# One product of seven by a second level of Strassen's scheme in the gate and up stage of a gated MLP

## The chip, the cores and the metric

The kernel runs on one core of a Trainium2 chip. A core has five engines that run side by side, each through its own instructions in order: TensorE (PE in the profile; matmuls, and weight loads that overlap them), VectorE (DVE), ScalarE (ACT), GpSimd (POOL) and SyncE (SP, which issues transfers here). They wait for one another by semaphores. The metric is the device time of one run, in microseconds (us), lower is better.

## The reference

Two layers on x of 2048 rows and 1024 columns: a local attention, then a gated MLP. Only the second matters here (F = 3584):

```python
def _B_ref(x, w_gate, w_up, w_down):
    g = jnp.einsum("bsd,df->bsf", x, w_gate)
    u = jnp.einsum("bsd,df->bsf", x, w_up)
    h = g * u
    return jnp.einsum("bsf,fd->bsd", h, w_down)
...
h = x + _A_ref(_layernorm(x, axis=-1), A_wqkv, A_wo)
h2 = h + _B_ref(_layernorm(h, axis=-1), B_w_gate, B_w_up, B_w_down)
```

## The kernel before

The rows are cut into 4 chunks of 512 (TC). For chunks 0 and 1, gate and up are plain products. Chunks 2 and 3 are taken together, in 14 blocks (NP) of 256 columns of gate and of up each. In a block, for gate (i = 0) and for up (i = 1), the product of a 256 x 1024 piece of weights with the 1024 x 1024 activations of the two chunks is done by Strassen's scheme in Winograd's form: both are seen as 2 x 2 cells, and seven products of cells take the place of eight. A cell of weights is 128 x 512, a cell of activations 512 x 512, so that one such product is 4 matmuls of 128 x 128 weights with 512 columns, summed in one PSUM bank. Gate and up together are 14 products, or 56 matmuls, a block.

The sums of weight cells are made a block ahead. VectorE scales and converts the raw weights to f16 (`wt`), and GpSimd makes four sums for gate and four for up from them (`sw`). For the first block VectorE makes the sums. The sums of activation cells (t1 to t4) are made once. Names in the profile carry the tile and the block: `px`, `py`, `pz`, `pv` are PSUM banks of the products, `p` is p5, `hq...` and `up` are the results for gate and up, `ws` is `wt`, `prodx` holds t1 to t4.

```python
    def weight_sums(n, eng=nc.gpsimd):
        raw = pair["w", n]
        wt = wpool.tile([128, KO, 2, 256], F16, tag="w", name=f"ws_{n}")
        if n == 0:
            nc.scalar.activation(wt[:], raw[:], ACTF.Copy, scale=scale_gu.s)
        else:
            nc.vector.tensor_scalar(wt[:], raw[:], scale_gu.s, None, ALU.mult)
        sw = wpool.tile([128, 2, 4, 4, 128], F16, tag="w", name=f"sw_{n}")
        for i in ((slice(0, 2),) if eng is nc.vector else (slice(0, 1), slice(1, 2))):
            a11, a21, a12, a22 = (wt[:, k:k + 4, i, c:c + 128].rearrange("p k i c -> p i k c")
                                  for k in (0, 4) for c in (0, 128))
            eng.tensor_tensor(sw[:, i, 0], a21, a22, ALU.add)
            eng.tensor_tensor(sw[:, i, 1], sw[:, i, 0], a11, ALU.subtract)
            eng.tensor_tensor(sw[:, i, 2], a11, a21, ALU.subtract)
            eng.tensor_tensor(sw[:, i, 3], a12, sw[:, i, 1], ALU.subtract)
        pair["a", n], pair["s", n] = wt, sw
        state["live"] += 1

    def activation_sums(l2, l3, room):
        b11, b12, b21, b22 = l2[:, 0:4, :], l3[:, 0:4, :], l2[:, 4:8, :], l3[:, 4:8, :]

        t1, t2, t3, t4 = (room[:, bass.ts(i, 4), :].bitcast(F16) for i in range(4))
        nc.vector.tensor_tensor(t1, b12, b11, ALU.subtract)
        nc.vector.tensor_tensor(t2, b22, t1, ALU.subtract)
        nc.vector.tensor_tensor(t3, b22, b12, ALU.subtract)
        nc.vector.tensor_tensor(t4, b21, t2, ALU.subtract)
        pair["b"] = (b11, b21, t1, t2, t3, t4, b22)

    def product(ps, lhs, rhs, fresh):
        for ko in range(4):
            nc.tensor.matmul(ps[:], lhsT=lhs[:, ko, :], rhs=rhs[:, ko, :], start=(fresh and ko == 0),
                             stop=(ko == 3), skip_group_check=not fresh)

    def pair_block(n, hts, sums=()):
        b11, b21, t1, t2, t3, t4, b22 = pair["b"]
        wt, sw, inv = pair["a", n], pair["s", n], scale_gu.inv
        gu = range(2)
        out = [hts, [t1k.tile([128, TC], BF, tag="t1k", name=f"up{n}_{k}")[:] for k in range(4)]]

        def bank(k, i):
            return psum.tile([128, TC], F32, tag="mm", name=f"p{k}{n}_{i}")

        xb, yb, zb, vb, p5 = [[None] * 2 for _ in range(5)]
        for i in gu:
            xb[i] = bank("x", i)
            product(xb[i], wt[:, 0:4, i, 0:128], b11, True)
            yb[i] = bank("y", i)
            nc.scalar.copy(yb[i][:], xb[i][:])
        for i in gu:
            vb[i] = bank("v", i)
            product(vb[i], sw[:, i, 0], t1, True)
            p5[i] = att.tile([128, TC], F32, tag=("lg", "t3")[i], name=f"p5{n}_{i}")
            nc.scalar.activation(p5[i][:], vb[i][:], ACTF.Copy, scale=inv)
            product(yb[i], sw[:, i, 1], t2, False)
            zb[i] = bank("z", i)
            nc.scalar.copy(zb[i][:], yb[i][:])
        for i in gu:
            product(zb[i], sw[:, i, 2], t3, False)
            nc.vector.scalar_tensor_tensor(out[i][3], zb[i][:], inv, p5[i][:], ALU.mult, ALU.add)
            product(xb[i], wt[:, 4:8, i, 0:128], b21, False)
            nc.scalar.activation(out[i][0], xb[i][:], ACTF.Copy, scale=inv)
            for k in sums[2 * i:2 * i + 2]:
                k()
        for i in gu:
            product(zb[i], wt[:, 4:8, i, 128:256], t4, False)
            nc.scalar.activation(out[i][2], zb[i][:], ACTF.Copy, scale=inv)
            product(yb[i], sw[:, i, 3], b22, False)
            nc.vector.scalar_tensor_tensor(out[i][1], yb[i][:], inv, p5[i][:], ALU.mult, ALU.add)
        for k in (3, 0, 2, 1):
            nc.vector.tensor_tensor(out[0][k], out[0][k], out[1][k], ALU.mult)
        state["live"] -= 2
```

The scheme runs on three partial results that are passed on: x, then y (a copy of x plus the t2 product), then z (a copy of that y plus the t3 product). The product `v` (`sw[:, i, 0]` with t1) goes into SBUF as p5 and is added when a result that needs it leaves PSUM. The loop around it:

```python
    for n in range(NP):
        if n + 1 < NP:
            weight_sums(n + 1)
            if n + 2 < NP:
                load_pair(n + 2)
            else:
                names = ("b11a", "b12a", "b21a", "b21b", "b12b")
                ws = {k: home(wpool, "w", "dn_" + k, BF) for k in names}
                down["b11"] = [ws["b11a"], home(att, "oD", "dn_b11b", BF)]
                down["b12"] = [ws["b12a"], ws["b12b"]]
                down["b21"] = [ws["b21a"], ws["b21b"]]
                load_down(down["b11"], 0, 0)
                load_down(down["b12"], 0, 1)
        else:
            load_down(down["b21"], 1, 0)
        sums = [] if n == 0 else [
            (lambda n=n, k=k: abs_sum_h(n - 1, k, h23[4 * (n - 1) + k])) for k in range(4)]
        pair_block(n, h23[4 * n:4 * n + 4], sums)
        if n == NP - 2:
            conv_down(down["b11"])
```

A buffer pool hands a place out again when the last reader of it is done. An engine that needs a place waits for that reader.

Of the kernel before, what the change touches and what calls it, by code (L numbers as in the profile page):

```python
# [9 lines left out]
F32 = mybir.dt.float32  # L10
I32 = mybir.dt.int32
F16 = mybir.dt.float16
ALU = mybir.AluOpType
ACTF = mybir.ActivationFunctionType
# [11 lines left out]
TC = 512  # L26
NCH = S // TC
SUB = TC // 4
KO = D // 128
NF = F // 128  # L30
NP = NF // 2
# [47 lines left out]
def kernel(  # L79
# [11 lines left out]
    nc = tc.nc  # L91
    x = A_x.flatten_outer_dims()
# [12 lines left out]
    att = ctx.enter_context(tc.tile_pool(name="att", bufs=1))  # L105
# [687 lines left out]
    pair = {}  # L793
# [8 lines left out]
# [5 lines that stand above are left out]
        else:  # L807
            nc.vector.tensor_scalar(wt[:], raw[:], scale_gu.s, None, ALU.mult)
        sw = wpool.tile([128, 2, 4, 4, 128], F16, tag="w", name=f"sw_{n}")
        for i in ((slice(0, 2),) if eng is nc.vector else (slice(0, 1), slice(1, 2))):  # L810
            a11, a21, a12, a22 = (wt[:, k:k + 4, i, c:c + 128].rearrange("p k i c -> p i k c")
                                  for k in (0, 4) for c in (0, 128))
            eng.tensor_tensor(sw[:, i, 0], a21, a22, ALU.add)  # L813
            eng.tensor_tensor(sw[:, i, 1], sw[:, i, 0], a11, ALU.subtract)  # L814
            eng.tensor_tensor(sw[:, i, 2], a11, a21, ALU.subtract)  # L815
            eng.tensor_tensor(sw[:, i, 3], a12, sw[:, i, 1], ALU.subtract)  # L816
        pair["a", n], pair["s", n] = wt, sw
        state["live"] += 1

# [10 lines left out]
    def product(ps, lhs, rhs, fresh):  # L830
        for ko in range(4):
            nc.tensor.matmul(ps[:], lhsT=lhs[:, ko, :], rhs=rhs[:, ko, :], start=(fresh and ko == 0),  # L832
                             stop=(ko == 3), skip_group_check=not fresh)

    def pair_block(n, hts, sums=()):
        b11, b21, t1, t2, t3, t4, b22 = pair["b"]
        wt, sw, inv = pair["a", n], pair["s", n], scale_gu.inv
# [4 lines that stand above are left out]
            return psum.tile([128, TC], F32, tag="mm", name=f"p{k}{n}_{i}")  # L842

        xb, yb, zb, vb, p5 = [[None] * 2 for _ in range(5)]
        for i in gu:
            xb[i] = bank("x", i)
            product(xb[i], wt[:, 0:4, i, 0:128], b11, True)
            yb[i] = bank("y", i)
            nc.scalar.copy(yb[i][:], xb[i][:])  # L849
        for i in gu:  # L850
            vb[i] = bank("v", i)
            product(vb[i], sw[:, i, 0], t1, True)
            p5[i] = att.tile([128, TC], F32, tag=("lg", "t3")[i], name=f"p5{n}_{i}")
            nc.scalar.activation(p5[i][:], vb[i][:], ACTF.Copy, scale=inv)
            product(yb[i], sw[:, i, 1], t2, False)
            zb[i] = bank("z", i)
            nc.scalar.copy(zb[i][:], yb[i][:])
        for i in gu:
            product(zb[i], sw[:, i, 2], t3, False)
            nc.vector.scalar_tensor_tensor(out[i][3], zb[i][:], inv, p5[i][:], ALU.mult, ALU.add)  # L860
            product(xb[i], wt[:, 4:8, i, 0:128], b21, False)
            nc.scalar.activation(out[i][0], xb[i][:], ACTF.Copy, scale=inv)
            for k in sums[2 * i:2 * i + 2]:
                k()
        for i in gu:
            product(zb[i], wt[:, 4:8, i, 128:256], t4, False)
            nc.scalar.activation(out[i][2], zb[i][:], ACTF.Copy, scale=inv)
            product(yb[i], sw[:, i, 3], b22, False)
            nc.vector.scalar_tensor_tensor(out[i][1], yb[i][:], inv, p5[i][:], ALU.mult, ALU.add)
        for k in (3, 0, 2, 1):  # L870
            nc.vector.tensor_tensor(out[0][k], out[0][k], out[1][k], ALU.mult)
        state["live"] -= 2
# [239 lines left out]
    b11, b21 = ([wts["dn", n, a] for a in range(2)] for n in ("11", "21"))  # L1112

    def halves(parts, name):
        return [pool.tile([128, KO, TC], BF, tag=tag, name=f"{name}{i}") for i, (pool, tag) in enumerate(parts)]

    b12 = halves(((att, "qD"), (att, "kD")), "b12")
    a21 = halves(((lnTp, "lnT"), (lnTp, "lnT")), "a21")
    a22 = halves(((lnTp, "lnT"), (wpool, "w")), "a22")
# [121 lines left out]
    b22 = halves(((lnTp, "lnT"), (wpool, "w")), "b22")  # L1241
# [15 lines left out]
    t2 = halves(((wpool, "w"), (wpool, "w")), "t2_")  # L1257
# [5 lines left out]
    for q in range(4):  # L1263
        ev = psum.tile([128, TC], F32, tag="mm", name=f"ev{q}")
        dprod(ev, q, FS1, fcells(b11), True)
        p = lnp.tile([128, TC], F32, tag="ln", name=f"ep5_{q}")
# [7 lines left out]
    room = wpool.tile([128, 4, TC], F32, tag="w", name="hsr0")  # L1274
# [4 lines left out]
    b21 = halves(((lnTp, "lnT"), (lnTp, "lnT")), "b21r")  # L1279
# [10 lines left out]
    a22 = halves(((att, "vD"), (att, "oD")), "a22r")  # L1290
# [42 lines left out]
    t4 = t2  # L1333
# [11 lines left out]
    retire(2)  # L1345
    load_pair(1)
    weight_sums(0, nc.vector)
    for q in range(4):
        dprod(zs[q], q, F22, fcells(t4), False)
# [20 lines left out]
# [20 lines that stand above are left out]
# [16 lines left out]
    for q in range(4):  # L1406
        dprod(ps_x[q], q, HA["11"], fcells(down["b11"]), True)
        if q == 1:
            scale_h.total(ps_y[3])
            inv = const.tile([128, 1], F32, name="inv_hd")  # L1410
            nc.vector.tensor_tensor(inv[:], scale_h.inv, scale_d.inv, ALU.mult)
            inv = inv[:]
# [26 lines left out]
    p5 = []  # L1439
    for q in range(4):  # L1440
        dprod(ps_x[q], q, S1, fcells(t1h), True)
        p = lnp.tile([128, TC], F32, tag="ln", name=f"dp5_{q}")
# [60 lines left out]
```

## Time and profile before

| | us |
|---|---|
| median of 3 runs | 766.32 |
| lowest and highest | 766.16, 766.51 |
| span of the profiled run | 764.4 |
| PE busy | 756.2 |
| VectorE busy | 627.9 |
| ScalarE busy | 531.5 |
| GpSimd busy | 144.9 |

How to read the views that follow. A line of groups or of the timeline has the engine, the line of the kernel (L), the operation, what it writes and reads (`out<-in`), partitions x elements and type. In the timeline the first two numbers are the start and the length in us, neighbours of one kind are merged (x4), and square brackets tell how long the engine had been idle before, and who ended that. A row of windows gives the busy time of each engine in a stretch. The matmuls of a stream overlap: one with 512 columns is recorded with 379 ns, and the next starts 215.8 ns after it. So it is the spacing of the starts, not the recorded length, that says what a matmul costs.

The stage that is changed begins at 506.6 us (first `px`) and its last product is issued by 675.9 us, where the first `dx` product of the down stage starts.

### The profile page before, as it was taken

To read this page: it belongs to the slowest core of one execution; us is meant where nothing else is said; L and a number is where in the kernel's file an instruction comes from. 1 tells how busy PE (TensorE), PEld (TensorE's weight loads), DVE (VectorE), ACT (ScalarE), POOL (GpSimd) and SP (SyncE) were. 2 spreads that over 40 slices of the span, in tenths; PEclk is the share of its full clock that TensorE was granted. 3 is DMA by queue.
4 is the path that set the end of the run, shared out by engine and by line. 5 is a ranking of instruction groups with operands and counts; after the bars stand their busy time and mean duration, and the time that the engine had idled before them with its cause. 6 is when DMAs were issued, how large, how long until landed. Compare 5 with 4: busy or idle time off the path is not lost.

```text
span 764.4 us, 10272 instructions
## 1 busy us (share of the span) xinstructions
PE 756.2 (99%) x3576; PEld 348.0 (46%) x3632; DVE 627.9 (82%) x758; ACT 531.5 (70%) x1010; POOL 144.9 (19%) x155
## 2 busy tenths in 40 slices
PE   8999999999999999999999999999999999999998
PEld 6444444444444444444444444444444444444444
DVE  6879999999999999999999999976554453578862
ACT  4756864556799598997798984846767677788230
POOL 0010000200002000010000001018778778600000
PEclk9999999999999999999999999999999999999999
DMA  8999695967998959879768528684242332830001
GB/s 272 255 237 263 183 287 131 301 191 172 343 345 283 302 178 294 271 245 336 245 214 275 174 95 280 150 206 128 57 110 62 105 94 72 275 112 27 1 28 55
DMA packets 194099, 146.29 MB, mean 191 GB/s; under 512 B 83968, under 2 KB 184192, under 8 KB 192000
## 3 DMA queue, kind: packets, MB, share of 16 engines
q1 hardware_dynamic: 184640, 117.99, 54.6%
q0 software_dynamic: 3728, 22.02, 8.4%
q10 hardware_dynamic: 5680, 5.64, 2.3%
q8 instruction: 28, 0.46, 0.2%
q14 instruction: 23, 0.19, 0.1%
HBM read 111.02 MB, written 27.26 MB: 181 GB/s over the span
## 4 chain that ended last, share of the span: by engine, by line
PE 86%; DVE 8%; ACT 2%; DMA 1%; issue 1%; ACTq 0%; DVEq 0%; SPq 0%
PE ps L474 17%; PE dx L1093 6%; PE pz L832 6%; PE pwu L474 6%; PE py L832 6%; PE px L832 6%; PE pwg L474 6%; PE wo L1147 4%; PE pv L832 3%; PE ey L1093 3%; PE ez L1093 3%; PE ex L1093 3%; PE dy L1093 3%; PE pu L474 2%; PE pg L474 2%; DVE prod L531 2%
## 5 line engine op out<-in xcount | busy, mean ns | idle before, releaser
L474 PE MATMUL ps<-lnT,w_qkv 128*128 128x512 bf16 x595 | 131.1, 379 | 0.7
L474 PEld LDWEIGHTS <-w_qkv 128*128 128x128 bf16 (+1 forms) x608 | 59.3, 98 | 71.5
L531 DVE TENSOR_TENSOR prod<-qD,kD 128x4096 bf16<-128x4096 bf16 (+1 forms) x34 | 72.3, 2160 | 4.0 <-DMA kD<-kd 4.0
L579 DVE TENSOR_TENSOR pv<-vD,at 128x4096 bf16<-128x4096 bf16 x32 | 72.4, 2286 | 0.3
L832 PEld LDWEIGHTS <-sw 128*128 128x128 f16 x448 | 43.8, 98 | 53.0 <-issue 0.2
L474 PEld LDWEIGHTS <-w_wg 128*128 128x128 bf16 x448 | 43.8, 98 | 52.9
L474 PEld LDWEIGHTS <-w_wu 128*128 128x128 bf16 x448 | 43.7, 98 | 52.9
L388 ACT CAST sg<-ps 128x512 bf16<-128x512 f32 x72 | 41.6, 584 | 30.7 <-PE ps L474 26.1
L832 PE MATMUL px<-lnT,ws 128*128 128x512 bf16 x212 | 53.1, 379 | 0.6
L474 PE MATMUL pg<-lnT,w_wg 128*128 128x512 bf16 x219 | 52.7, 379 | 0.3
L474 PE MATMUL pwu<-lnT,w_wu 128*128 128x512 bf16 x220 | 52.6, 379 | 0.3
L474 PE MATMUL pu<-lnT,w_wu 128*128 128x512 bf16 x220 | 52.6, 379 | 0.2
L474 PE MATMUL pwg<-lnT,w_wg 128*128 128x512 bf16 x219 | 52.3, 379 | 0.2
L832 PEld LDWEIGHTS <-ws 128*128 128x128 f16 x336 | 32.8, 98 | 39.7
L592 POOL DMA_DIRECT2D od<-oD x4 | 2.2, 542 | 249.4 <-DVE oD L590 249.4
L813 POOL TENSOR_TENSOR sw<-ws 128x512 f16<-128x512 f16 x26 | 30.0, 1153 | 78.4 <-PE pz L832 47.2
L1093 PEld LDWEIGHTS <-gs 128*128 128x128 f16 (+1 forms) x280 | 27.3, 98 | 33.2 <-DVE gs L1261 0.5
L533 DVE TENSOR_TENSOR prod<-prod 128x4096 bf16<-128x4096 bf16 x16 | 36.6, 2288 | 0.3
L849 ACT COPY py<-px 128x512 f32<-128x512 f32 x28 | 16.0, 570 | 24.2 <-PE px L832 24.2
L816 POOL TENSOR_TENSOR sw<-ws,sw 128x512 f16<-128x512 f16 x26 | 30.7, 1182 | 0.0
L814 POOL TENSOR_TENSOR sw<-sw,ws 128x512 f16<-128x512 f16 x26 | 30.0, 1154 | 2.0
L815 POOL TENSOR_TENSOR sw<-ws 128x512 f16<-128x512 f16 x26 | 30.2, 1161 | 0.0
(367 smaller groups left out, 1574.0 us busy)
## 6 DMA issues: line engine op xcount, KB each, us to landing
w_wg<-in_B_w_gate_dram SPq DMA_DIRECT2D x14, 1024.0 KB, 6.3
w_wu<-in_B_w_up_dram SPq DMA_DIRECT2D x14, 1024.0 KB, 9.6
w_pair<-in_B_w_gate_dram SPq DMA_DIRECT2D x14, 512.0 KB, 4.0
w_pair<-in_B_w_up_dram SPq DMA_DIRECT2D x14, 512.0 KB, 5.2
w_wo<-in_A_wo_dram SPq DMA_DIRECT2D x6, 1024.0 KB, 7.9
w_qkv<-in_A_wqkv_dram SPq DMA_DIRECT2D x5, 1024.0 KB, 9.7
kd<-sg SPq DMA_DIRECT2D x32, 144.0 KB, 4.3
vd<-sg SPq DMA_DIRECT2D x32, 144.0 KB, 2.5
```

Source lines behind the costliest of these rows:

```text
L388: nc.scalar.copy(sg[:, HB:HB + TC], ps[:])
L474: nc.tensor.matmul(ps[:], lhsT=wt[:, ko, bass.ts(j, 128)], rhs=rhs[:, ko, :], start=(ko == 0), stop=(ko == KO - 1))
L531: nc.vector.tensor_tensor(prod[:, j, ds], qD[:, ds], kD[:, ds, o:o + SUB], ALU.mult)
L533: nc.vector.tensor_tensor(prod[:, :, 0:16], prod[:, :, 0:16], prod[:, :, 16:32], ALU.add)
L579: nc.vector.tensor_tensor(pv[:, j], vD[:, :, o:o + SUB], at[:, w, None, :].to_broadcast((128, DH, SUB)), ALU.mult)
L813: eng.tensor_tensor(sw[:, i, 0], a21, a22, ALU.add)
L814: eng.tensor_tensor(sw[:, i, 1], sw[:, i, 0], a11, ALU.subtract)
L815: eng.tensor_tensor(sw[:, i, 2], a11, a21, ALU.subtract)
L816: eng.tensor_tensor(sw[:, i, 3], a12, sw[:, i, 1], ALU.subtract)
L832: nc.tensor.matmul(ps[:], lhsT=lhs[:, ko, :], rhs=rhs[:, ko, :], start=(fresh and ko == 0), stop=(ko == 3), skip_group_check=not fresh)
L1093: nc.tensor.matmul(ps[:, bass.ds(lo, n)], lhsT=lhs[k][:, bass.ts(q, 128)], rhs=rhs[k][:, bass.ds(lo, n)], start=(fresh and k == 0), stop=( ...
L1147: nc.tensor.matmul(ps[:], lhsT=oTs[c][:, kk, t, :], rhs=wts["wo", 2, hf][:, kk, :], start=(kk == 0), stop=(kk == KO - 1))
```

## The change

In blocks 1 to 13 the product `v` of gate and `v` of up, two half products of seven, are seen as one: the cell sums `sw[:, 0, 0]` of gate and `sw[:, 1, 0]` of up are the two row halves of a 256 x 512 matrix, which is multiplied with t1 (512 x 512). On this one product the scheme is used once more. Its cells are 128 x 256 and 256 x 256, so that a small product is 2 matmuls with 256 columns, and there are seven of them in place of the 8 products of cells (8 matmuls with 512 columns). It is meant to take work off PE.

For this it needs:

- sums of cells of t1, once (`inner_rows`, on VectorE, in block 0);
- sums of the cells of `sw[:, :, 0]`, for every block (`inner_weights`, on VectorE, placed in the block before, between the two reads of the last `y` products);
- two PSUM banks, each shared by two small results: lx and lv, ly and lz;
- copies and scaled reads of 256 columns between the small products, on ScalarE, and two on VectorE, which write the second halves of p5;
- GpSimd's sums in another order: the first sum of gate and of up, then the second of both, and so on, because the first ones are now inputs of further sums.

The new small products are spread among the large ones, `inner(...)` in the diff. A small product with `False` as its last argument adds to what stands in PSUM, where its columns hold something. Otherwise nothing is changed: block 0 is done as before, and so are all other stages.

```diff
--- before.py
+++ after.py
@@ -807,13 +807,14 @@
         else:
             nc.vector.tensor_scalar(wt[:], raw[:], scale_gu.s, None, ALU.mult)
         sw = wpool.tile([128, 2, 4, 4, 128], F16, tag="w", name=f"sw_{n}")
-        for i in ((slice(0, 2),) if eng is nc.vector else (slice(0, 1), slice(1, 2))):
-            a11, a21, a12, a22 = (wt[:, k:k + 4, i, c:c + 128].rearrange("p k i c -> p i k c")
-                                  for k in (0, 4) for c in (0, 128))
-            eng.tensor_tensor(sw[:, i, 0], a21, a22, ALU.add)
-            eng.tensor_tensor(sw[:, i, 1], sw[:, i, 0], a11, ALU.subtract)
-            eng.tensor_tensor(sw[:, i, 2], a11, a21, ALU.subtract)
-            eng.tensor_tensor(sw[:, i, 3], a12, sw[:, i, 1], ALU.subtract)
+        a11, a21, a12, a22 = (wt[:, k:k + 4, :, c:c + 128].rearrange("p k i c -> p i k c")
+                              for k in (0, 4) for c in (0, 128))
+        both = (slice(0, 2),)
+        each = both if eng is nc.vector else (slice(0, 1), slice(1, 2))
+        for j, x, y, op in ((0, a21, a22, ALU.add), (1, sw[:, :, 0], a11, ALU.subtract), (2, a11, a21, ALU.subtract),
+                            (3, a12, sw[:, :, 1], ALU.subtract)):
+            for i in each:
+                eng.tensor_tensor(sw[:, i, j], x[:, i], y[:, i], op)
         pair["a", n], pair["s", n] = wt, sw
         state["live"] += 1
 
@@ -832,6 +833,33 @@
             nc.tensor.matmul(ps[:], lhsT=lhs[:, ko, :], rhs=rhs[:, ko, :], start=(fresh and ko == 0),
                              stop=(ko == 3), skip_group_check=not fresh)
 
+    def inner_rows(t):
+        room = att.tile([128, KO, TC], F16, tag="vD", name="inner_t")
+        b11, b12, b21, b22 = (t[:, k:k + 2, c:c + 256] for k in (0, 2) for c in (0, 256))
+        t1, t2, t3, t4 = (room[:, i, :].rearrange("p (k c) -> p k c", k=2) for i in range(4))
+        nc.vector.tensor_tensor(t1, b12, b11, ALU.subtract)
+        nc.vector.tensor_tensor(t2, b22, t1, ALU.subtract)
+        nc.vector.tensor_tensor(t3, b22, b12, ALU.subtract)
+        nc.vector.tensor_tensor(t4, b21, t2, ALU.subtract)
+        pair["iv"] = room[:, 4, :].bitcast(F32)
+        pair["ib"] = (b11, b21, t1, t2, t3, t4, b22)
+
+    def inner_weights(n):
+        sw = pair["s", n]
+        a11, a12, a21, a22 = (sw[:, i, 0, k:k + 2, :] for i in range(2) for k in (0, 2))
+        room = att.tile([128, 4, 2, 128], F16, tag="at", name=f"inner_w{n}")
+        s1, s2, s3, s4 = (room[:, i] for i in range(4))
+        nc.vector.tensor_tensor(s1, a21, a22, ALU.add)
+        nc.vector.tensor_tensor(s2, s1, a11, ALU.subtract)
+        nc.vector.tensor_tensor(s3, a11, a21, ALU.subtract)
+        nc.vector.tensor_tensor(s4, a12, s2, ALU.subtract)
+        pair["ia", n] = (a11, a12, a22, s1, s2, s3, s4)
+
+    def inner(ps, lhs, rhs, fresh):
+        for k in range(2):
+            nc.tensor.matmul(ps, lhsT=lhs[:, k, :], rhs=rhs[:, k, :], start=(fresh and k == 0), stop=(k == 1),
+                             skip_group_check=not fresh)
+
     def pair_block(n, hts, sums=()):
         b11, b21, t1, t2, t3, t4, b22 = pair["b"]
         wt, sw, inv = pair["a", n], pair["s", n], scale_gu.inv
@@ -842,24 +870,52 @@
             return psum.tile([128, TC], F32, tag="mm", name=f"p{k}{n}_{i}")
 
         xb, yb, zb, vb, p5 = [[None] * 2 for _ in range(5)]
+        nested = ("ia", n) in pair
+        if nested:
+            a11, a12, a22, s1, s2, s3, s4 = pair["ia", n]
+            c11, c21, r1, r2, r3, r4, c22 = pair["ib"]
+            first, last = bank("i", 0), bank("i", 1)
+            lx, lv = (first[:, bass.ts(i, 256)] for i in range(2))
+            ly, lz = (last[:, bass.ts(i, 256)] for i in range(2))
+            v5 = pair["iv"]
         for i in gu:
+            p5[i] = att.tile([128, TC], F32, tag=("lg", "t3")[i], name=f"p5{n}_{i}")
             xb[i] = bank("x", i)
             product(xb[i], wt[:, 0:4, i, 0:128], b11, True)
             yb[i] = bank("y", i)
             nc.scalar.copy(yb[i][:], xb[i][:])
+            if nested and i == 0:
+
+                inner(lx, a11, c11, True)
+                inner(lv, s1, r1, False)
+                nc.scalar.activation(v5, lv, ACTF.Copy, scale=inv)
+                nc.scalar.copy(ly, lx)
         for i in gu:
-            vb[i] = bank("v", i)
-            product(vb[i], sw[:, i, 0], t1, True)
-            p5[i] = att.tile([128, TC], F32, tag=("lg", "t3")[i], name=f"p5{n}_{i}")
-            nc.scalar.activation(p5[i][:], vb[i][:], ACTF.Copy, scale=inv)
+            if not nested:
+                vb[i] = bank("v", i)
+                product(vb[i], sw[:, i, 0], t1, True)
+                nc.scalar.activation(p5[i][:], vb[i][:], ACTF.Copy, scale=inv)
             product(yb[i], sw[:, i, 1], t2, False)
             zb[i] = bank("z", i)
             nc.scalar.copy(zb[i][:], yb[i][:])
+            if nested and i == 0:
+                inner(ly, s2, r2, False)
+                inner(lx, a12, c21, False)
+                nc.scalar.copy(lz, ly)
+                nc.scalar.activation(p5[0][:, 0:256], lx, ACTF.Copy, scale=inv)
+        if nested:
+            inner(lz, s3, r3, False)
+            inner(ly, s4, c22, False)
+            nc.vector.scalar_tensor_tensor(p5[0][:, 256:512], ly, inv, v5, ALU.mult, ALU.add)
+            nc.vector.scalar_tensor_tensor(p5[1][:, 256:512], lz, inv, v5, ALU.mult, ALU.add)
         for i in gu:
             product(zb[i], sw[:, i, 2], t3, False)
             nc.vector.scalar_tensor_tensor(out[i][3], zb[i][:], inv, p5[i][:], ALU.mult, ALU.add)
             product(xb[i], wt[:, 4:8, i, 0:128], b21, False)
             nc.scalar.activation(out[i][0], xb[i][:], ACTF.Copy, scale=inv)
+            if nested and i == 0:
+                inner(lz, a22, r4, False)
+                nc.scalar.activation(p5[1][:, 0:256], lz, ACTF.Copy, scale=inv)
             for k in sums[2 * i:2 * i + 2]:
                 k()
         for i in gu:
@@ -867,6 +923,10 @@
             nc.scalar.activation(out[i][2], zb[i][:], ACTF.Copy, scale=inv)
             product(yb[i], sw[:, i, 3], b22, False)
             nc.vector.scalar_tensor_tensor(out[i][1], yb[i][:], inv, p5[i][:], ALU.mult, ALU.add)
+            if i == 0 and n + 1 < NP:
+                if n == 0:
+                    inner_rows(t1)
+                inner_weights(n + 1)
         for k in (3, 0, 2, 1):
             nc.vector.tensor_tensor(out[0][k], out[0][k], out[1][k], ALU.mult)
         state["live"] -= 2
```

## The prediction

> **What bounds the kernel now.** I read the busy shares first, then the stage that the change touches, cut into its 14 blocks, then what TensorE (PE), VectorE (DVE) and GpSimd (POOL) do inside single blocks.
>
> ```profile
> PE 756.2 (99%) x3576; PEld 348.0 (46%) x3632; DVE 627.9 (82%) x758; ACT 531.5 (70%) x1010; POOL 144.9 (19%) x155
> ```
>
> PE is the bound of the whole kernel. In the gate and up stage of chunks 2 and 3 (about 506.6 to 675.9 us) it is the bound without any gap:
>
> ```profile
> core 0: us, PE busy (x) PEld busy (x) DVE busy (x) ACT busy (x) POOL busy (x), PEclk, DMA share, GB/s
> 603.50:615.60 12.10, 12.05 (x57) 5.48 (x56) 5.54 (x9) 8.62 (x18) 9.15 (x9) 1.00 0.33 87
> 615.60:627.70 12.10, 12.05 (x57) 5.47 (x56) 5.53 (x9) 8.62 (x18) 9.03 (x9) 1.00 0.32 87
> ```
>
> A block starts every 12.085 us (the chain has them at 603.53, 615.61, 627.70), and 12.085 / 56 matmuls is 215.8 ns each: no wait at all. DVE, ScalarE (ACT) and POOL have room on average. What counts is when they work. In a late and in an early block:
>
> ```profile
> 651.26 1.15 POOL L816 TENSOR_TENSOR sw<-ws,sw 128x512 f16<-128x512 f16 x1
> ...
> 651.91 0.75 DVE L869 SCALAR_TENSOR_TENSOR up<-py,ibgu,p 128x512 bf16<-128x512 f32 x1 [0.97 <-PE py L832]
> 652.58 1.42 DVE L871 TENSOR_TENSOR hq_l<-hq_l,up 128x512 bf16<-128x512 bf16 x4
> 653.92 1.28 DVE L808 TENSOR_SCALAR ws<-w_pair,sbgu 128x4096 f16<-128x4096 bf16 x1
> ```
>
> ```profile
> 518.90 1.15 POOL L814 TENSOR_TENSOR sw<-sw,ws 128x512 f16<-128x512 f16 x1
> 520.01 1.33 POOL L815 TENSOR_TENSOR sw<-ws 128x512 f16<-128x512 f16 x1
> 521.31 1.33 POOL L816 TENSOR_TENSOR sw<-ws,sw 128x512 f16<-128x512 f16 x1
> ...
> 519.63 3.64 DVE L871 TENSOR_TENSOR hq<-hq,up 128x512 bf16<-128x512 bf16 x4
> 523.19 1.27 DVE L808 TENSOR_SCALAR ws<-w_pair,sbgu 128x4096 f16<-128x4096 bf16 x1
> ```
>
> This is the pair of rows on which my prediction rests. The same four DVE products take 1.42 us when POOL has just finished (651.26 + 1.15 = 652.41) and 3.64 us when POOL still works. In the slow case the second and third start at 520.26 and 521.56: a spacing of 1.30 us in place of 0.34, which is one POOL sum. POOL in turn takes 1.33 in place of 1.15. The two alternate. The PSUM reads of L869 and L860 take 0.75 us whether POOL works or not.
>
> **What the Trainium skill says.** "SBUF — State Buffer", section "Who interferes with whom": VectorE and GpSimd share one pair of SBUF ports under an exclusive lock, held for a whole instruction; a tensor_tensor with both inputs in SBUF contends with GpSimd's reads, an instruction with at most one SBUF input outside the two-port modes does not. The trace agrees on both: 1.30 against 0.34 us for L871, 0.75 always for L860 and L869. "TensorE: Matmul & The Clock Gate", section "Back-to-back issue gap", gives N/2.4 + 2.5 ns warm for N columns; the trace has 215.8 ns at 512, and for shorter ones:
>
> ```profile
> 757.93 1.14 PE L1093 MATMUL dy<-dn_b22a,hq 128*128 128x384 f16 x6
> 758.91 0.33 PE L1093 MATMUL dy<-dn_b22a,hq_q 128*128 128x384 f16 x1
> ...
> 760.21 0.50 PE L1093 MATMUL dx<-dn_b22a,hq 128*128 128x128 f16 x6
> 760.54 0.22 PE L1093 MATMUL dx<-dn_b22a,hq_q 128*128 128x128 f16 x1
> ```
>
> That is (758.91 - 757.93)/6 = 163 ns at 384 and (760.54 - 760.21)/6 = 55 ns at 128, each with its own weight load. So 256 columns, between these two, cost 109 ns, and the weight load (98 ns, overlapped) does not bind.
>
> **What it removes.** In 13 blocks, two products of 4 matmuls with 512 columns: 8 x 215.8 = 1.726 us. **What it adds on PE:** 7 small products of 2 matmuls with 256 columns: 14 x 109 = 1.528 us. Saved: 0.198 us a block, 2.6 us in all, the block being 11.89 us. This is all that there is to win.
>
> **What it adds elsewhere.** ACT: five passes of 256 columns for two of 512, estimated at 2.1 us against 1.4 (687 ns each before); it has 3.5 us to spare in a block. DVE: two PSUM reads of 256 columns (p5's second halves), about 0.4 us each by half of L860's slope, and one SBUF input, so POOL does not disturb them; and four sums of 128x256 in f16 for the next block's weights (estimated 0.2 to 0.33 us each, from 0.34 for 512 and 0.60 for 1024). In block 0 also four sums of 128x512 for the rows. POOL has the same 8 sums, in another order.
>
> The four weight sums stand between the two reads of y (L869), where DVE idled 0.97 us, and undisturbed they would fit (about 1.0 us). But that place is 11.1 us into the block, and POOL works on until about 13.6 (its sums start at 643.24 and 655.33, 3.5 us into the blocks of 639.79 and 651.87, and end at 652.41). All have two SBUF inputs. So each waits for a POOL sum.
>
> **The new path.** DVE is in order: y1's read, four products, the conversion of the weights to come, p5's two reads. PE's last small product (lz with a22) writes where the second p5 read reads, so it waits for it. By PE's order alone it stands 6 x 0.863 + 6 x 0.218 = 6.49 us into the block. Call E the end of y1's read. Then: products 1.3, conversion 1.2, p5 reads 0.8, hand-over 0.15, so PE can go on at E + 3.45. E may be 3.0 us into the block without harm; before it is 0.95.
>
> From there one turn of the loop: lz and four products (z1, x1, z0, y0) 0.22 + 4 x 0.863 = 3.67; result to DVE 0.20 (the timeline has y0's last product issued by 577.46 and its read at 577.66); y0's read 0.67: the weight sums begin at E + 8.0. POOL, which waits for the conversion, began at E + 2.55 and has a sum every 1.11 us: three or four of eight are left. The DVE sums take turns with them and the fourth ends near E + 11.75 (to 12.05), when POOL is done; y1's read adds 0.75. A turn is 12.5 to 12.8 us where PE alone needs 11.89. So the loop through DVE is the bound, and the block is 0.4 to 0.7 us longer than before.
>
> **The sum.** Block 0's end: POOL's sums run from 513.1 to about 522.0 without the gaps. DVE's first row sum starts at 517.90; the four take turns with POOL until 522.8, the weight sums follow by 523.8, E is 524.6 in place of 519.7. PE's second small product in block 1 needs the first row and weight sums: it waits from 519.8 to 523.2. The next E is 537.4, and eleven more turns at 12.65 bring 676.6. In block 13 the wait stands behind two conversions of the down weights (2.1 us in place of 1.2): PE goes on at 676.6 + 3.45 + 0.9 = 681.0 and has 5.4 us left: 686.3 against 675.9. What follows is as before, moved by 10.4 us: 766.3 + 10.4 = 776.7.
>
> **Rivals.** (1) The saving comes through: POOL yields, or the sums slip between its instructions. Then the wait never rises, at most block 1 pays 1 us for the row sums, and the time is about 764.5. For it: PE has no wait today, and the order of POOL's sums was changed so that the inputs are early. Against it: the 3.64 us row, where each product but the last lost its turn. I give it one in ten. (2) Every sum loses a whole turn and the delays add to POOL's work (1.33 in place of 1.15): a turn of 13.1 us, 4.5 us more, 782. Rather less likely than the middle. (3) ACT becomes the bound, with copies between small products: lz's copy is ready about 0.15 us before PE wants it by my working, so a few tenths a block, 2 to 3 us on top of (1), 767; where DVE is late anyway it is hidden. (4) Weight loads bind the 256-column products: the 55 ns spacing at 128 columns speaks against it.
>
> **Range and chances.** 776.5, the middle of the loop's two ends. The range of 768 to 783 holds from a turn with only two sums losing (about 12.2 us) to one with all four. Faster by 2% would be 751 and more than the change removes. Slower by 2% is 781.6, near rival 2: one in eight. The rest lies within.
>
> **What would show it.** Right: the new weight sums on DVE (128x256) at 0.5 to 1.3 us each, not 0.28; blocks of 12.5 to 12.8 us and PE idle 0.6 to 0.9 in each, put down to DVE's p5 reads; a wait of about 3 us in block 1; DVE behind PE in the chain; 256-column matmuls every 109 ns. Wrong: sums of 0.28 us and blocks of 11.9 us (rival 1), PE waits for ACT (3), or small matmuls spaced wider (4).

## The result and the profile after

| | us |
|---|---|
| before, median of 4 runs | 766.24 (766.04 to 766.51) |
| after, median of 4 runs | 775.47 (775.37 to 776.01) |
| after / before | 1.0122, 95% interval 1.0104 to 1.0139 |

The kernel became 9.2 us slower. The stage of chunks 2 and 3 took 178.43 us (first `px` to first `dx`, 506.87 to 685.31) in place of 169.29: that is 9.14 us, so nothing of note happens elsewhere. First the busy shares of the page:

```profile
PE 760.5 (98%) x3710; PEld 356.9 (46%) x3710; DVE 676.8 (87%) x840; ACT 537.5 (69%) x1049; POOL 144.8 (19%) x155
```

VectorE's busy time grew by 48.9 us. One small thing stands out in it: the 52 weight sums (4 for each of 13 blocks), recorded with 47.0 us in all, though one of them takes 0.28 us undisturbed. Two blocks, from first `px` to first `px`, with the columns of the same view of before:

```profile
core 0: us, PE busy (x) PEld busy (x) DVE busy (x) ACT busy (x) POOL busy (x), PEclk, DMA share, GB/s
603.58:616.15 12.57, 12.05 (x63) 6.07 (x62) 10.02 (x16) 9.16 (x22) 9.09 (x9) 1.00 0.31 84
616.15:628.71 12.56, 12.05 (x62) 6.07 (x62) 10.02 (x16) 9.15 (x22) 9.08 (x9) 1.00 0.31 85
```

A block is now 12.56 us, while PE's busy share has a hole of half a microsecond in each. What fills the hole is listed by the waits of PE over the stage (in total, times, longest):

```profile
PE pi L860 <- DVE p L910: 5.9, 10, 1.4
PE pi L860 <- DVE inner_w L852: 2.5, 1, 2.5
```

Before, this stage had no such line. The first is ten small products that wait for the second p5 read, the second is the wait in block 1. The view counts from the recorded end of the matmul before; counted from the moment at which the next matmul was due by the spacing of the starts, each wait is about 0.16 us longer. The chain of waits through the end of one block and on into the next shows why the p5 read is late (start, length, what):

```profile
641.28 0.38 PE pi L860 x2
641.66 0.86 PE pz L833 x4
642.52 0.86 PE px L833 x4
643.39 0.86 PE pz L833 x4
644.25 0.88 PE py L833 x4
645.13 0.03 issue
645.15 0.75 DVE hq_l L925
645.90 0.44 DVE inner_w L852
646.34 0.02 issue
646.37 1.12 DVE inner_w L853
647.49 1.16 DVE inner_w L854
648.65 1.16 DVE inner_w L855
649.81 0.66 DVE up L925
...
651.73 1.28 DVE ws L808
653.01 0.39 DVE p L909
653.40 0.40 DVE p L910
653.81 0.04 issue
653.85 0.38 PE pi L860 x2
```

It begins and ends with the same small product (lz with a22), 12.57 us apart: this is the loop, and 3.9 us of it are the four weight sums. GpSimd in the same stretch of the timeline:

```profile
645.02 2.32 POOL L817 TENSOR_TENSOR sw<-ws 128x512 f16<-128x512 f16 x2
647.31 2.35 POOL L817 TENSOR_TENSOR sw<-ws,sw 128x512 f16<-128x512 f16 x2
```

These are its last four sums, at about 1.16 us each. VectorE's four end at 646.34, 647.49, 648.65 and 649.81: the steps are again 1.15 to 1.16 us. One VectorE sum gets in behind each GpSimd sum, the last when GpSimd is done.

The 14 blocks differ, and that matters further down (us, before: 12.16, then 12.09 each):

| block | 0 | 1 | 2 | 3 | 4 | 5 to 12 | 13 |
|---|---|---|---|---|---|---|---|
| after | 12.16 | 16.16 | 11.89 | 11.89 | 12.32 | 12.56 to 12.57 | 13.50 |

Against before, block 1 alone loses 4.1 us, blocks 5 to 12 together 3.8 and block 13 1.4; blocks 2 and 3 save 0.4.

### The profile page after: what moved, and what is told of

It reads as the page before. It is cut to its first block, busy times and chain, and to the rows that moved or that the text cites. A ratio compares the mean times of both kernels' runs of the same rounds, so it can differ in the third digit from the quotient of the medians.

```text
span 773.8 us, 10621 instructions
## 1 busy us (share of the span) xinstructions
PE 760.5 (98%) x3710; PEld 356.9 (46%) x3710; DVE 676.8 (87%) x840; ACT 537.5 (69%) x1049; POOL 144.8 (19%) x155
## 5 line engine op out<-in xcount | busy, mean ns | idle before, releaser
L833 PE MATMUL px<-lnT,ws 128*128 128x512 bf16 x224 | 58.2, 384 | 0.0
L833 PEld LDWEIGHTS <-sw 128*128 128x128 f16 x344 | 33.9, 98 | 33.0 <-issue 1.3
L833 PE MATMUL py<-prodx,sw 128*128 128x512 f16 x112 | 29.3, 385 | 0.0
```

## The experiments

My theory: it is VectorE's turn-taking with GpSimd, at a place that a p5 read and behind it PE wait for. Rivals: the added work as such (more instructions on VectorE, ScalarE and PE), the new order of GpSimd's sums, or contention that slows the stage wherever it falls. The runs of before that stood beside each group gave medians of 766.32 to 766.44 us.

### The sums made once

The weight sums are made for block 1 alone and used again in all others. 48 of the 52 sums are left out, so that blocks 2 to 13 work with sums that are not theirs; all else runs as in the changed kernel.

```diff
+        if n > 1:
+            pair["ia", n] = (a11, a12, a22) + pair["once"]
+            return
         room = att.tile([128, 4, 2, 128], F16, tag="at", name=f"inner_w{n}")
         s1, s2, s3, s4 = (room[:, i] for i in range(4))
+        pair["once"] = (s1, s2, s3, s4)
```

> The changed kernel, but the four weight sums for the small products are made for block 1 alone and used in all later blocks (the output is then not that of the reference; it is a measure of time). Block 1 and its wait are untouched. Theory (the sums lose turns to GpSimd's sums, so y1's read and all behind it on VectorE come late): blocks 2 to 13 at 11.89 us without a wait, the stage about 171 us, total 768.0 us (767.5 to 768.5). Rival (the small products themselves, their copies on ScalarE or their weight loads hold PE up, whatever VectorE does): blocks stay above 12.3 us, total 773 to 776.

Measured: 768.16 us, ratio 1.0020 (1.0011 to 1.0028); the single times lie in two groups, which the last section comes back to. Blocks 2 to 13 all take 11.89 us, which is the block that PE needs by itself; block 1 takes 16.19. So the small products, the copies on ScalarE and the p5 reads cost nothing: their rival falls. What is left over before is block 1.

### The sums there, but with one input in PSUM

As many sums, in the same place, but the second input of each is read from the bank of y, in PSUM. The values are not the scheme's.

```diff
+        other = ps[:, 0:256].rearrange("p (k c) -> p k c", k=2)
-        nc.vector.tensor_tensor(s1, a21, a22, ALU.add)
+        nc.vector.tensor_tensor(s1, a21, other, ALU.add)
...
-                inner_weights(n + 1)
+                inner_weights(n + 1, yb[0])
```

> The changed kernel with the four weight sums in the same place and number, but with the second input read from the y bank in PSUM in place of SBUF, so each has one SBUF input (the values are then not those of the scheme, and the output is not the reference's). Theory (the port shared with GpSimd): each sum takes about 0.48 us although alone it is slower than the 0.28 us of an undisturbed f16 sum, never 1.1; blocks 2 to 13 at 11.89 us; total 768.0 us (767.5 to 769). Rival (four more instructions in that place are too many, or their dependency on GpSimd's semaphore holds VectorE): total as the changed kernel, 774 to 776.

Measured: 767.98 us, ratio 1.0017 (1.0010 to 1.0024). The timeline of VectorE in a late block, and of GpSimd beside it:

```profile
642.99 0.41 DVE L853 TENSOR_TENSOR inner_w<-sw,py 128x256 f16<-128x256 f16 x1
643.43 0.42 DVE L854 TENSOR_TENSOR inner_w<-inner_w,py 128x256 f16<-128x256 f16 x1
643.77 0.41 DVE L855 TENSOR_TENSOR inner_w<-sw,py 128x256 f16<-128x256 f16 x1
644.11 0.41 DVE L856 TENSOR_TENSOR inner_w<-sw,py 128x256 f16<-128x256 f16 x1
```

```profile
642.65 2.26 POOL L817 TENSOR_TENSOR sw<-ws,sw 128x512 f16<-128x512 f16 x2
```

GpSimd works through all of it, at 1.13 us a sum, and VectorE's four are done in 1.5 us. Blocks 2 to 13 take 11.89 us. So it is not the number of instructions nor GpSimd's being busy, but the second input in SBUF. (The type of that input changed with its place, f32 in place of f16. Undisturbed, an f16 sum is recorded with 0.28 us; with the PSUM input it is longer than that, and yet nothing is lost.) The Trainium skill, "SBUF — State Buffer", section "Who interferes with whom", says this of one SBUF input against two, and here a sum in this place has 0.41 us against up to 1.24.

### The sums as dead work

The kernel before with GpSimd's new order and the four weight sums in their place, but nothing uses them: v is made by 8 matmuls as before, and there is no p5 read on VectorE. From the diff against the changed kernel:

```diff
             yb[i] = bank("y", i)
             nc.scalar.copy(yb[i][:], xb[i][:])
-            if nested and i == 0:
-                inner(lx, a11, c11, True)
...
-            if not nested:
-                vb[i] = bank("v", i)
-                product(vb[i], sw[:, i, 0], t1, True)
+            vb[i] = bank("v", i)
+            product(vb[i], sw[:, i, 0], t1, True)
...
-                if n == 0:
-                    inner_rows(t1)
                 inner_weights(n + 1)
```

> The kernel before, with GpSimd's new order of sums and with the four weight sums on VectorE in the same place as in the changed kernel, but as dead work: nothing uses them, v is done as before by 8 matmuls of 512 columns, and no p5 read stands on VectorE. My theory (the sums cost only because a p5 read waits behind them and a small product behind that): the sums take 1.1 to 1.3 us each while GpSimd works, y1's read ends 3 us later, yet blocks stay at 12.09 us and the time at 766.3 (765.5 to 767.5). Rival (the turn-taking by itself slows the stage, or the new order of GpSimd's sums does): blocks of 12.5 us or more, 772 to 777 us.

Measured: 766.36 us, ratio 1.0002 (0.9993 to 1.0010). VectorE's timeline in one of its blocks:

```profile
627.00 0.45 DVE L841 TENSOR_TENSOR inner_w<-sw 128x256 f16<-128x256 f16 x1
627.49 1.13 DVE L842 TENSOR_TENSOR inner_w<-inner_w,sw 128x256 f16<-128x256 f16 x1
628.54 1.24 DVE L843 TENSOR_TENSOR inner_w<-sw 128x256 f16<-128x256 f16 x1
629.70 1.24 DVE L844 TENSOR_TENSOR inner_w<-sw,inner_w 128x256 f16<-128x256 f16 x1
630.86 0.74 DVE L881 SCALAR_TENSOR_TENSOR up<-py,ibgu,p 128x512 bf16<-128x512 f32 x1
```

The sums are as slow as in the changed kernel (55.7 us for all 52, 47.0 there), y1's read ends 3.6 to 4.6 us into the block in place of 0.95, and every block is still 12.09 us. Here contention alone costs nothing, and neither does GpSimd's new order: PE pays where something that it needs soon stands behind the sums.

### GpSimd makes the sums

The four weight sums are made by GpSimd, behind its two first sums, and are gone from their place on VectorE (one of the four is shown).

```diff
+            if n > 0 and j == 0:
+                inner_weights(n, sw)
...
-        nc.vector.tensor_tensor(s1, a21, a22, ALU.add)
+        nc.gpsimd.tensor_tensor(s1, a21, a22, ALU.add)
```

> The four weight sums of a block are made by GpSimd, right behind its two first sums, in place of VectorE. My theory (what costs is VectorE's turn-taking with GpSimd ahead of the second p5 read, whichever engine has the extra sums): GpSimd now works some 11.3 us of a block (8 x 1.15 + 4 x about 0.5), so VectorE's four products behind y1's read fall into its work and take turns, 3.6 us in place of 1.4. The second p5 read comes 1.5 to 3 us later and blocks stay at 12.4 to 13.5 us: 775 to 788 us. Rival (four instructions fewer on VectorE end the trouble): blocks of 11.9 us, 764 to 768 us.

Measured: 789.06 us, ratio 1.0295 (1.0279 to 1.0310), 1 us above the range of the theory. Blocks 3 to 12 take 13.56 to 13.62 us, block 13 16.19. Again VectorE's timeline, from y1's read on:

```profile
629.22 0.75 DVE L926 SCALAR_TENSOR_TENSOR up<-py,ibgu,p 128x512 bf16<-128x512 f32 x1 [0.97 <-PE py L835]
629.89 4.38 DVE L930 TENSOR_TENSOR hq_o<-hq_o,up 128x512 bf16<-128x512 bf16 x4
634.19 2.17 DVE L808 TENSOR_SCALAR ws<-w_pair,sbgu 128x4096 f16<-128x4096 bf16 x1
```

GpSimd now works until 635.27, and the four products, 1.42 us in the changed kernel, take 4.38. PE waits for the second p5 read 13 times, 20.5 us in all. What I had not counted is the conversion: 2.17 us in place of 1.28, although it has one SBUF input. It waits too. (The section of the Trainium skill named above lists tensor_scalar among the instructions that can take the shared ports in their fast modes; that fits.) The sums were moved off VectorE, and its busy time rose all the same, from 676.8 to 680.0 us.

### The sums ahead of y0's read

VectorE idled 1.4 us ahead of y0's read. Here the row and weight sums are put there.

```diff
             product(yb[i], sw[:, i, 3], b22, False)
-            nc.vector.scalar_tensor_tensor(out[i][1], yb[i][:], inv, p5[i][:], ALU.mult, ALU.add)
             if i == 0 and n + 1 < NP:
                 if n == 0:
                     inner_rows(t1)
                 inner_weights(n + 1)
+            nc.vector.scalar_tensor_tensor(out[i][1], yb[i][:], inv, p5[i][:], ALU.mult, ALU.add)
```

> The changed kernel with the row sums and the weight sums moved in VectorE's order from behind y0's read to ahead of it, where VectorE idles 1.8 us and another 1.0 us follows. Computes the reference. Theory: the sums still take 1.1 to 1.3 us each, VectorE busy time is the same, but y1's read ends about 2.3 us into the next block, under the 3.0 that does no harm: blocks 2 to 12 at 11.89 us, block 13 at most 0.3 more, block 1 still waits 3 to 4 us; total 767 to 768.5 us. Rival (what counts is how long the sums take, not where they stand): blocks of 12.5 us again, 774 to 776.

Measured: 766.38 us, ratio 1.0001 (0.9993 to 1.0010). This is 0.6 us below the range of the theory, which had PE wait 3 to 4 us in block 1; the block loses 2.4. Blocks 2 to 12 take 11.89 us, block 13 12.15, block 1 14.26. The 52 weight sums together take 53.0 us, *more* than in the changed kernel. Only their place is better.

### The row sums too, ahead of the stage's first conversion

Against the run with the sums ahead of y0's read:

```diff
             if i == 0 and n + 1 < NP:
-                if n == 0:
-                    inner_rows(t1)
                 inner_weights(n + 1)
...
     down = {}
+    inner_rows(pair["b"][2])
     for n in range(NP):
```

> As the one before, and the four row sums made ahead of the stage's first conversion, when GpSimd does not work yet. Computes the reference. Theory: row sums 0.4 us each, block 1 waits under 0.8 us, PE idle nearly nowhere in the stage, which is about 167 us; total 764.0 us (763.5 to 765), under the kernel before by 2.2. Rival: the wait in block 1 is that for the first weight sum itself and stays over 2 us, 766 to 767.

Measured: 765.15 us, ratio 0.9985 (0.9978 to 0.9992): the first version that beats before, and 1.2 us short of what I expected. Block 1 still takes 13.17 us: PE waits 1.05 us there, for a p5 read.

### The row sums alone moved

The weight sums stay between the two y reads; the row sums go ahead of the first conversion. This asks why blocks 2 and 3 of the changed kernel were not slow.

> The changed kernel with the row sums alone moved, ahead of the first conversion of the stage; the weight sums stay between the two y reads. My theory (the loop through VectorE binds from block 2 on; blocks 2 to 4 of the changed kernel were short only because the long wait in block 1 had put GpSimd ahead): block 1 loses about 1 us instead of 4, blocks 2 to 12 take 12.5 to 12.6 us from the first on, block 13 about 13.5: 773.3 to 774.7 us. Rival (the loop binds only after some blocks for a reason of its own, such as buffers): blocks 2 and 3 at 11.9 us again, 771.5 to 772.7 us.

Measured: 774.05 us, ratio 1.0101 (1.0084 to 1.0118). Block 1 takes 12.94 us, block 2 12.51, blocks 3 and 4 12.65, the rest 12.56, block 13 13.49. Over the stage:

```profile
PE pi L860 <- DVE p L910: 8.1, 13, 1.4
```

Thirteen waits in place of ten, and none for the row sums: the loop binds from block 1 on. The rival falls. The reason that my expectation gave for the short blocks was not exact; the traces show this. Let E be the end of y1's read, as in the prediction. In the changed kernel PE was so late in block 1 that E stood only 1.7 us into block 2. The sums made in blocks 0 to 3 met one GpSimd sum more each time (1.1, 2.0, 2.9 and 3.9 us for the four), so that E crept 0.9 us further into each block (1.7, 2.6, 3.6 us in blocks 2 to 4), until it passed 3 us and PE had to wait. Here E is 3.9 us into block 1 from the beginning.

This run and the one before it differ in the place of the weight sums alone, and that gives the plainest comparison of all: 774.05 us with 53.6 us of sums between the two y reads, 765.15 us with 55.2 us of the same sums ahead of y0's read.

### The sums in gaps, and the way to the best version

The weight sums are spread over three idle places of VectorE, the row sums stay ahead of the first conversion, and half of the first down weights is converted inside block 13. `inner_weights` now stops after each sum, and `next(steps, None)` makes the next one.

```diff
     for i in gu:
         product(zb[i], sw[:, i, 2], t3, False)
         nc.vector.scalar_tensor_tensor(out[i][3], zb[i][:], inv, p5[i][:], ALU.mult, ALU.add)
+        for _ in range(1 + i):
+            next(steps, None)
+        if i and n == NP - 1:
+            conv_down(down["b11"][1:])
```

> The whole scheme, with the row sums ahead of the first conversion of the stage, the weight sums split over VectorE's gaps (one behind the first z read, two behind the second, one behind y0's read), and half of the first down weights converted inside block 13, behind the z reads. My theory: nothing on VectorE then delays the second p5 read: blocks 1 to 13 of 11.9 us but for at most 0.5 us in block 1, and 763.9 to 764.8 us. Rival (a part of the loss does not come from where the sums stand): 765.2 us or more, no better than with both kinds of sums ahead of y0's read.

Measured: 765.05 us, ratio 0.9983 (0.9976 to 0.9990), so the number of my theory was missed, and the gain over sums ahead of y0's read is nil, as the rival had it. Its blocks: 1 to 13 all 11.89, but block 0 takes 13.48. The first sum there waits until 516.70 for GpSimd's second sum and, VectorE being in order, z1's read stands behind it; PE idles 1.33 us. The gain was lost at another place. The last version leaves block 1 on the old scheme and makes no weight sums in block 0:

```diff
-        steps = inner_weights(n + 1) if n + 1 < NP else iter(())
+        steps = inner_weights(n + 1) if 0 < n < NP - 1 else iter(())
```

> As in the run with the sums in the gaps, but the second level begins in block 2, so that no weight sums are made in block 0, where the first of them waited for GpSimd's second sum and held up the second z read (TensorE then idled 1.33 us there). My theory (that idle time is all that was lost in that run): block 0 back at 12.16 us, block 1 at 12.09, blocks 2 to 13 at 11.89: 12 x 0.198 = 2.4 us saved, 763.9 us (763.5 to 764.4). Rival (something else in block 0 or 1 costs, for example the row sums ahead of the conversion, which start GpSimd 1.4 us later): 764.8 to 765.3 us.

Measured: 764.23 us against 766.44, ratio 0.9972 (0.9961 to 0.9982). The stage, in windows of a block each:

```profile
core 0: us, PE busy (x) PEld busy (x) DVE busy (x) ACT busy (x) POOL busy (x), PEclk, DMA share, GB/s
605.00:616.89 11.89, 11.84 (x63) 6.06 (x63) 10.30 (x17) 8.83 (x22) 9.14 (x8) 1.00 0.33 89
616.89:628.78 11.89, 11.84 (x63) 6.08 (x63) 9.97 (x16) 8.83 (x22) 9.16 (x8) 1.00 0.34 93
```

Blocks 2 to 13 take 11.89, block 1 12.26: there the first weight sum holds up z1's read once more, and PE loses 0.17 us. VectorE is as busy as in the changed kernel (10.0 to 10.3 us a block), and from block 2 on PE waits for nothing. It saves 2.2 us of the 2.4 that twelve blocks can give, and has the lowest median of all versions.

## Why the prediction was right, point by point

**PE's saving.** 0.198 us a block was predicted, a block of 11.89; the runs without the loop have 11.89 in place of 12.09. Small products of 256 columns start every 109 ns, as worked out (in the PE rows below, two products of two matmuls start at 526.33 and 526.55); the rival of binding weight loads falls. The Trainium skill, "TensorE: Matmul & The Clock Gate", section "Back-to-back issue gap", gives the formula that the prediction takes from it for a matmul by itself, and other figures, 131 ns at 512 columns and 81 ns at 128, for a stream with weight loads. The streams here have 215.8 and 55 ns, so the measurement decides for the formula.

**ScalarE.** Five short passes were put at 2.1 us; they take 0.48 + 0.39 + 0.36 + 0.49 + 0.47 = 2.2. It is no bound: that rival falls with the 11.89 us of the runs above.

**The weight sums.** 0.5 to 1.3 us each was predicted; in the steady state they take 0.51, 1.13, 1.23 and 1.24. The rival in which all is saved falls here, and the one with a whole turn lost by each is met in part: four sums end behind four GpSimd sums, but the first arrives in the middle of one and so waits only the rest of it, and GpSimd's own sums grow to about 1.16 us, not to 1.33.

**The loop**, from E on:

| | predicted | measured |
|---|---|---|
| GpSimd's first sum starts | E + 2.55 | E + 2.67 (637.91 to 640.58) |
| PE goes on with lz | E + 3.45 | E + 3.38 (650.47 to 653.85) |
| y0's read ends, sums begin | E + 8.0 | E + 7.99 |
| fourth weight sum ends | E + 11.75 to 12.05 | E + 11.90 |
| turn | 12.5 to 12.8, middle 12.65 | 12.56 to 12.57 |
| PE idle in a block | 0.6 to 0.9 | 0.68 |

**Block 0 to 1.** VectorE's timeline, with the row sums and the first weight sums, and PE's next to it:

```profile
518.17 0.45 DVE L840 TENSOR_TENSOR inner_t<-prodx 128x512 f16<-128x512 f16 x1
518.66 1.26 DVE L841 TENSOR_TENSOR inner_t<-prodx,inner_t 128x512 f16<-128x512 f16 x1
519.84 1.37 DVE L842 TENSOR_TENSOR inner_t<-prodx 128x512 f16<-128x512 f16 x1
521.13 1.37 DVE L843 TENSOR_TENSOR inner_t<-prodx,inner_t 128x512 f16<-128x512 f16 x1
522.42 0.28 DVE L852 TENSOR_TENSOR inner_w<-sw 128x256 f16<-128x256 f16 x1
```

```profile
519.89 0.38 PE L860 MATMUL pi<-prodx,sw 128*128 128x256 f16 x2
522.76 0.61 PE L860 MATMUL pi<-inner_t,inner_w 128*128 128x256 f16 x2 [2.48 <-DVE inner_w L852]
...
526.33 0.38 PE L860 MATMUL pi<-inner_t,inner_w 128*128 128x256 f16 x2
526.55 0.38 PE L860 MATMUL pi<-prodx,sw 128*128 128x256 f16 x2
```

The row sums take turns until 522.5 (predicted 522.8), the weight sums, with GpSimd done, take 0.28 each, and E is 524.10 (predicted 524.6). PE waits 2.65 us (the product at 522.76 was due at 520.11), not 3.4.

**The sum.** The stage was to end at 686.3 and ended at 685.3. The difference: the first E came 0.5 us earlier; the next turn was 12.81 as predicted (12.8); the eleven turns after it took 138.70 us in place of 139.15, so 0.45 less; from the last E to the first product of the down stage 9.70 us passed, predicted 9.75.

**Where a step was wrong.** The prediction has the loop "the bound" from its first turn at 12.65 us. For PE it was not: blocks 2 and 3 ran at their own 11.89 us, without a wait. That the sum came out all the same is partly luck of the counting. E's turns there were 12.80 and 12.81 us, because the sums grew by a lost turn each, and it is E that the end hangs on; the long block 1 paid in advance for what the blocks after it did not. The run with the row sums moved shows it: block 1 is 3.2 us shorter (12.94 for 16.16), but the time falls by only 1.4 us, 1.15 of which is the earlier first E (522.95 for 524.10).

Two of its figures are slips. GpSimd's work in the kernel before ends 12.6 us into the block (652.41 - 639.79), not 13.6. So at the place of the sums, 11.1 us in, only 1.5 us of it are left, and "each waits for a POOL sum" does not hold from the start: as measured, one sum in block 1 lost its turn, two in block 2, three in block 3. The loop was worked out from E and not from this figure, and its steady turn came out. And in rival (2), eleven turns of 13.1 in place of 12.65 us are 5.0 us more, not 4.5.

**Block 13.** The two conversions were to add 0.9 us to its wait; it is 1.61 us for 0.68, so 0.93.

## What to carry to other kernels

Before VectorE gets new two-input work in SBUF, look at what GpSimd does at that moment: a sum of 0.28 us costs a GpSimd instruction of 1.16 us there. That was harmless as long as nothing that the bounding engine soon waits for stood behind it in VectorE's order, so look for the place, not for the shortest work: the same sums, of about the same length, made a difference of 9 us by their place alone. And the first and the last turn of a loop (inputs still being made, other work let in) can eat half of a small saving: here the first was left on the old scheme and part of the other work was moved out of the way of the last.

## What the runs showed of the hardware that was not expected

After the wait of 2.65 us in block 1, PE ran at half clock. The windows of the changed kernel have it in the column PEclk, ahead of the DMA share:

```profile
520.50:522.70 2.20, 0.00 (x0) 0.00 (x0) 2.20 (x3) 0.22 (x1) 1.72 (x2) 0.99 1.17 324
522.70:524.60 1.90, 1.84 (x6) 0.89 (x7) 1.87 (x7) 0.75 (x2) 0.00 (x0) 0.50 0.37 89
524.60:526.30 1.70, 1.70 (x6) 0.55 (x4) 1.70 (x4) 0.57 (x1) 0.00 (x0) 0.57 0.00 0
526.30:529.00 2.70, 2.70 (x18) 1.64 (x17) 1.00 (x3) 1.80 (x4) 2.29 (x3) 1.00 0.00 0
```

Matmuls of 512 columns start every 427 ns there, in place of 216, from 523.2 to 526.1: about 1.6 us are lost. The Trainium skill, "TensorE: Matmul & The Clock Gate", section "What's actually happening", puts the halving after an idle window of about 3.4 us; here 2.65 us were enough, and, by the clocks, in some executions only. The executions with the sums made once lie in two groups: four from 766.32 to 767.15 us with a mean clock of 0.999 or 1.0, eight from 768.04 to 770.07 with 0.996 to 0.999. The profiled one, with a wait of 2.6 us and the half clock behind it, is of the second group; that the first group had the wait without the half clock is inferred, as it has no trace. A wait of 1.6 us (block 13, and block 1 with the sums ahead of y0's read) brought no half clock in the profiled runs. In the changed kernel the lost 1.6 us hardly show at the end: without them, as in the run with the row sums moved, E's next turn is 12.81 us too. That they are hidden there is argued from this, not measured by itself.
